# Placing turns and laid rows between the last modes' products, and sending the last rows of all batches but the first by DMA

## The chip, the cores and the metric

The kernel runs on one core of one Trainium2 chip. The metric is device time in microseconds (us), the median of several executions. Engines: PE multiplies matrices, DVE and ACT move and change data, POOL issues the loads of weights and the small copies, SP issues the output.

## The reference, cut to what matters

```python
# sliding-window attention, 8 batches x 8 heads x 576 rows x 64 -> x [8, 576, 512]
X = rfft(x, axis=1)                       # first 64 modes are kept
Yr = Xr[m] @ w_r[m] - Xi[m] @ w_i[m]      # per mode m: two 512 x 512 weights
Yi = Xr[m] @ w_i[m] + Xi[m] @ w_r[m]
y = irfft(Y, n=576, axis=1)
u = x + y
out = u + relu(u @ w_ch)                  # w_ch 512 x 512
```

The weights of the 64 modes are 134 MB in float32. They are read once, and the transfer casts them to bfloat16 (512 KB each in memory on the chip).

## The kernel before

Modes 0 to 59 go through `mode()`. The last four, 60 to 63, are treated apart so that little remains to be done after the last weight: their products go to `psl`, eight rows a batch. The spectrum of each batch is 128 rows: 96 early ones, 24 *middle rows* (modes 48 to 59) and 8 *last rows* (modes 60 to 63). A *turn* (`turned`) multiplies such rows by `w_ch` into `psw` and transposes them into `psa`. In the closing stage each of 36 output tiles gets a *laid row* (`lay`: an identity product that puts the channel product of x into PSUM), a product with `yw`, a relu on ACT, a product with `Yb`, and an addition on DVE. `idle` products compute nothing that is used; they keep PE streaming, for the sake of its clock.

```python
def turned(lhs, m, psa, psw):
    for e in range(NC):
        nc.tensor.matmul(out=psw[:m, :], lhsT=lhs(e), rhs=wch[:, e, :], start=(e == 0), stop=(e == NC - 1))
    for e in range(NC):
        nc.tensor.transpose(out=psa[:m, e, :], in_=lhs(e), identity=ident_r)
# ... cut ...
        for b0, nb in ((2, 4), (6, 2)):                     # middle rows, all before the last modes
            psa = ...; psw = ...                            # one buffer each
            turned(lambda e: view(YTl, (e * B + b0) * R, [[1, R * nb]]), R * nb, psa, psw)
            for i in range(nb):                             # DVE empties psa, ACT empties psw
                nc.vector.tensor_copy(out=pair_tile("Yb", b0 + i)[E0:], in_=...)
                nc.scalar.copy(out=pair_tile("yw", b0 + i)[E0:], in_=...)
        for n in range(EARLY_ROWS):                         # 5
            lay(n)
        for m in range(ME, NM):                             # modes 60 to 63
            last_mode(m, wr, 0, 0, NC)                      # 16 products
            idle(5 if m < NM - 1 else 3)
            last_mode(m, wi, 1, 0, NC)                      # 16 products
            if m < NM - 1:
                idle(5)
# ... cut: closing stage: YT2 <- psl, one turn of batches 0 and 1 and the last rows of 2 to 7 ...
        RELU = 3
        for n in range(RELU):
            rectify(n)                                      # product with yw, relu
        for n in range(NQ):
            finish(n)                                       # product with Yb, addition, output
            if n < 2:
                spread(n)                                   # ACT copies psw / psa to yl, DMA to batches 2 to 7
            if n + RELU < NQ:
                rectify(n + RELU)
            if EARLY_ROWS <= n + RELU + 1 < NQ:
                lay(n + RELU + 1)
```

The softmax here doesn't subtract the row's maximum and nothing guards it: scores larger than these inputs give would overflow.

## Time and profile before

| | before |
|---|---|
| time, median of 3 (later 4) runs | 432.32 (432.34) us |
| last piece of the last weight has landed | 392.76 us |
| its last 16 products end (`psl` done) | 394.90 us |
| first product of the turn of the last rows | 395.56 us |
| first product of the closing stage | 397.41 us |
| PE's last product | 425.29 us |
| end of the span | 431.94 us |

Times inside a kernel are counted from the start of the profiled span. Landing times are the semaphore records of the trace: a load is landed when the last of its 16 engines has reported.

From the page: the span; the clock that PE was granted, in tenths of full speed; the busy share of the DMA engines. Both rows have 40 slices of 10.8 us.

```profile
span 431.9 us, 11402 instructions
...
PEclk9999999999998755555588998996566655569998
DMA  7999999999999999999999999999999999991897
```

DMA is above 90% in every slice from the 2nd to the 36th: until about 389 us the kernel is a stream of weights. After that comes the closing stage, which writes 9.4 MB.

PE in order of time, around the end of the stream (start, length, line, operation, output <- inputs; in brackets the idle time before and what ended it):

```profile
374.75 2.08 PE L678 MATMUL psw<-wch,YTl 128*128 128x512 f32 x4 [0.68 <-ACT YTl L58]
...
379.25 1.97 PE L678 MATMUL psw<-wch,YTl 128*64 128x512 f32 x4 [1.96 <-ACT yw L748]
...
383.69 0.68 PE L720 MATMUL psl<-XQ,wt 128*128 128x16 bf16 x16
384.21 1.37 PE L693 MATMUL psd<-x_sb,ident_bf 128*128 128x512 bf16 x5
...
394.27 0.63 PE L720 MATMUL psl<-XQ,wt 128*128 128x16 bf16 x16
...
397.41 0.96 PE L793 MATMUL pso<-yw,trigI 128*128 128x512 f32 x3 [0.39 <-ACT yw L777]
```

All turns and laid rows stand before 383.69. Then halves of last modes (16 products, 0.48 us to the next instruction) alternate with idle products (five take 1.08 us). None of the lines from 383.69 to 394.27 has a bracket, so PE waits for no weight there. The weights landed at these times, us:

```
mode 60: 375.46, 377.92   mode 61: 380.38, 382.89   mode 62: 385.29, 387.75
mode 63: 390.20, then the last weight in three pieces: 391.49, 392.11, 392.76
```

The last half starts 1.5 us after its data was complete. The chain of waits (start, length, what) says the same: after the load that ends at 373.03 there is no DMA left in it, only PE and, after `psl`, two copies one after the other.

```profile
355.11 17.92 DMA wt<-in_moe_w_i_dram
...
393.78 0.65 PE psd L693 x3
394.43 0.48 PE psl L720 x16
394.94 0.24 DVE YT L767
395.19 0.33 ACT YT L769
395.56 1.20 PE psw L678 x4
```

Stretches of the trace, here three: length, then busy time and count of PE, PE's weight loads, DVE, ACT and POOL, then the granted clock, the DMA share and GB/s.

```profile
387.92:391.33 3.41, 3.41 (x45) 2.06 (x44) 0.00 (x0) 0.00 (x0) 0.00 (x0) 1.00 0.73 128
391.33:394.75 3.42, 3.42 (x59) 2.30 (x56) 0.00 (x0) 0.00 (x0) 0.00 (x0) 1.00 0.06 11
410.00:415.00 5.00, 5.00 (x23) 4.05 (x22) 4.50 (x7) 3.72 (x8) 0.00 (x0) 1.00 1.01 376
```

With five idle products between halves PE is busy all of the time and the clock stays at 1.00. The third line is the closing stage: PE is busy throughout, but the DMA share is 1.01 too.

### The profile page before, as it was taken

The numbers are of one execution on the slowest core, as the hardware profiler recorded it, in microseconds if no ns is written. First come the engines' busy times: TensorE is split into PE (matmuls) and PEld (weight loads), VectorE is DVE, ScalarE is ACT, GpSimd is POOL, SyncE is SP. The second block draws the span as 40 slices with busy tenths as digits, with TensorE's granted clock in tenths as the row PEclk, the third lists the DMA queues.
The fourth block names the chain that finished last, engine by engine and source line by source line (L and its number), as shares of the span: only waits on it lengthen the run. The fifth ranks groups of instructions, "written<-read, shape, count | busy, mean of one in ns | idle before, by whom it ended". The sixth has DMA issues, their size and how long they took to land.

```text
span 431.9 us, 11402 instructions
## 1 busy us (share of the span) xinstructions
PE 314.1 (73%) x5080; PEld 224.1 (52%) x5080; DVE 163.1 (38%) x316; ACT 152.3 (35%) x263; POOL 96.8 (22%) x184
## 2 busy tenths in 40 slices
PE   6989999999989756122777978785265662488993
PEld 2555765666655656122566756553254541355782
DVE  5466765766663200307122322221011110032894
ACT  4485866866764120101122321221011110122872
POOL 7131231331020404212121212122102131200500
PEclk9999999999998755555588998996566655569998
DMA  7999999999999999999999999999999999991897
GB/s 143 212 213 213 214 213 213 213 212 213 214 214 202 190 214 216 254 214 213 214 213 213 214 214 213 213 214 213 214 213 214 214 209 214 214 210 29 263 367 267
DMA packets 31314, 92.17 MB, mean 213 GB/s; under 512 B 3392, under 2 KB 3648, under 8 KB 31264
## 3 DMA queue, kind: packets, MB, share of 16 engines
q0 software_dynamic: 26016, 82.00, 95.6%
q1 hardware_dynamic: 5248, 9.44, 6.2%
q8 instruction: 40, 0.66, 0.5%
q14 instruction: 10, 0.08, 0.1%
HBM read 162.53 MB, written 9.44 MB: 398 GB/s over the span
## 4 chain that ended last, share of the span: by engine, by line
DMA 43%; PE 39%; DVE 6%; issue 4%; ACT 3%; POOL 2%; DVEq 0%; POOLq 0%; ACTq 0%
DMA wt<-in_moe_w_r_dram 27%; DMA wt<-in_moe_w_i_dram 17%; PE pso L317 6%; PE pst L219 6%; PE pso L793 4%; PE psv L236 3%; PE psx L339 3%; DVE x_sb L325 2%; PE pss L372 2%; PE pss L273 2%; PE pso L714 2%; PE pss L292 2%; PE psy L551 2%; PE psy L546 2%; DVE vT L59 2%
## 5 line engine op out<-in xcount | busy, mean ns | idle before, releaser
L551 PE MATMUL psy<-XQ,wt 128*128 128x16 bf16 x784 | 48.1, 191 | 48.0 <-DMA wt<-in_moe_w_i_dram 46.4
L546 PE MATMUL psy<-XQ,wt 128*128 128x16 bf16 x832 | 52.3, 191 | 31.9 <-DMA wt<-in_moe_w_r_dram 31.3
L551 PEld LDWEIGHTS <-wt 128*128 128x128 bf16 x784 | 37.2, 104 | 54.2 <-DMA wt<-in_moe_w_i_dram 51.5
L546 PEld LDWEIGHTS <-wt 128*128 128x128 bf16 x832 | 39.6, 104 | 37.2 <-DMA wt<-in_moe_w_r_dram 36.0
L116 POOL DMA_DIRECT2D wt<-in_moe_w_i_dram x53 | 28.7, 542 | 101.1 <-DMA wt<-in_moe_w_i_dram 40.1
L572 PE MATMUL psz<-wch,xT 128*128 128x512 f32 x144 | 47.7, 474 | 1.0 <-DVE xT L569 1.0
L116 POOL DMA_DIRECT2D wt<-in_moe_w_r_dram x55 | 29.7, 539 | 78.8 <-DMA wt<-in_moe_w_r_dram 43.9
L569 DVE CAST xT<-pxt 128x512 fp32r<-128x512 bf16 x36 | 23.5, 687 | 62.4 <-PE pxt L566 62.4
L574 ACT CAST Z<-psz 128x512 fp32r<-128x512 f32 x36 | 21.1, 587 | 70.9 <-PE psz L572 70.8
L298 ACT ACTIVATE et<-pss 128x512 bf16<-128x512 f32 x72 | 39.2, 599 | 12.7 <-PE pss L292 12.6
L317 PE MATMUL pso<-vt,et 128*64 128x65 bf16 (+1 forms) x576 | 33.1, 204 | 4.3 <-DVE x_sb L325 4.2
L572 PEld LDWEIGHTS psz<-wch,xT 128*128 128x128 f32 x144 | 30.4, 226 | 7.2 <-issue 1.3
L317 PEld LDWEIGHTS <-et 128*64 128x64 bf16 (+1 forms) x576 | 22.9, 109 | 15.8 <-issue 7.8
L325 DVE TENSOR_TENSOR x_sb<-pso,rcp 128x640 bf16<-128x640 f32 x32 | 26.3, 822 | 0.9
L804 DVE TENSOR_TENSOR ot<-pso,x_sb 128x512 f32<-128x512 f32 x36 | 24.5, 691 | 2.5 <-PE pso L793 2.0
L59 DVE CAST YT<-psy 128x256 fp32r<-128x256 f32 x6 | 2.5, 423 | 59.8 <-PE psy L551 59.8
L798 ACT ACTIVATE pso<-pso 128x512 f32<-128x512 f32 x36 | 20.5, 582 | 5.4 <-PE pso L793 2.9
L273 PE MATMUL pss<-band,ident_bf 64*64 64x512 bf16 x160 | 19.9, 391 | 1.6 <-ACT et L298 1.6
L58 ACT CAST YT<-psy 128x256 fp32r<-128x256 f32 x6 | 2.2, 374 | 51.5 <-DVE YT L59 51.5
L59 DVE COPY vT<-pst 128x768 bf16<-128x768 bf16 x16 | 15.3, 958 | 13.4 <-PE pst L219 13.4
L686 DVE CAST Yb<-psa 96x512 fp32r<-96x512 f32 x8 | 5.5, 687 | 32.5 <-PE psa L680 32.5
L678 PE MATMUL psw<-wch,YT 128*96 128x512 f32 (+1 forms) x36 | 16.4, 601 | 0.7 <-ACT YT L769 0.7
(167 smaller groups left out, 509.0 us busy)
## 6 DMA issues: line engine op xcount, KB each, us to landing
wt<-in_moe_w_r_dram POOLq DMA_DIRECT2D x55, 512.0 KB, 19.1
wt<-in_moe_w_i_dram POOLq DMA_DIRECT2D x50, 512.0 KB, 19.1
out_dram<-ot SPq DMA_DIRECT2D x32, 256.0 KB, 3.2
rk<-in_k_dram POOLq DMA_DIRECT2D x8, 576.0 KB, 9.2
rq<-in_q_dram POOLq DMA_DIRECT2D x8, 576.0 KB, 13.3
rv<-in_v_dram POOLq DMA_DIRECT2D x8, 576.0 KB, 11.8
wy<-in_moe_w_i_dram POOLq DMA_DIRECT2D x4, 512.0 KB, 16.3
kT<-in_moe_w_i_dram POOLq DMA_DIRECT2D x2, 512.0 KB, 7.0
```

Of the source, the lines that this page charges most:

```text
L59: return nc.vector.tensor_copy(out=o, in_=i)
L116: nc.gpsimd.dma_start(out=wt[:, c0:c1], in_=src[m].rearrange("(p c) e -> p c e", c=NC)[:, c0:c1])
L219: nc.tensor.transpose(out=ps[64 * hh:64 * hh + 64, c, :], in_=src[:, hh, (c0 + c) * D:(c0 + c + 1) * D], identity=ident_bf)
L273: nc.tensor.matmul(out=pss[(2 * w + hh) % 3][64 * half:64 * half + 64, :], lhsT=ident_bf[pp, pp], rhs=view(band[pp], 128 * half, [[0, WIN ...
L298: nc.scalar.activation(out=et[:, hh, :], in_=pss[(2 * w + hh) % 3], func=ACT_F.Exp, scale=EX_SCALE)
L317: nc.tensor.matmul(out=pso[po, hh, (i // 2) * VW:(i // 2) * VW + D + 1], lhsT=et[pk, hh, col:col + 64], rhs=vt[pk, 1 - f % 2, 2 * hh + g / ...
L325: nc.vector.tensor_tensor(out=view(x_sb, b * NT * DM + g * D, [[4 * D, 2], [DM, NT], [1, D]]), in0=view(pso, 0, [[512, 2], [VW, NT], [1, D]]),
L546: nc.tensor.matmul(out=psy[:, m % MG, e, :], lhsT=wr[:, c, ee], rhs=XQ[:, c, :, 1:3, m], start=(c == 0), stop=(m == 0 and c == NC - 1))
L551: nc.tensor.matmul(out=psy[:, m % MG, e, :], lhsT=wi[:, c, ee], rhs=XQ[:, c, :, 0:2, m], start=False, stop=(c == NC - 1))
L569: nc.vector.tensor_copy(out=xT, in_=pst)
L572: nc.tensor.matmul(out=psz, lhsT=xT[:, c, :], rhs=wch[:, c, :], start=(c == 0), stop=(c == NC - 1))
L804: nc.vector.tensor_tensor(out=ot, in0=tps.pop(n), in1=x_sb[:, b, t, :], op=ALU.add)
```

## The change

The intent: let PE do turns and laid rows while it waits for weights, so that it is on time for the last one; make the step after `psl` shorter (one copy in place of two on different engines); take copies off ACT in the closing stage by treating batch 1 as batches 2 to 7; and load the last weight at once, as PE no longer needs its pieces. The number of idle products falls from 33 to 11.

```diff
@@ -112,8 +112,7 @@
         if wt is None:
             wt = pool.tile([128, NC, DM], BF16, name="wt", tag=tag)
         src = moe_w_i if im else moe_w_r
-        for c0, c1 in ((0, NC),) if i < NLOAD - 1 else ((0, 2), (2, 3), (3, 4)):
-            nc.gpsimd.dma_start(out=wt[:, c0:c1], in_=src[m].rearrange("(p c) e -> p c e", c=NC)[:, c0:c1])
+        nc.gpsimd.dma_start(out=wt, in_=src[m].rearrange("(p c) e -> p c e", c=NC))
         wtiles[m, im] = wt
 
     trigF = acons.tile([128, NT, 2 * NM], BF16, name="trigF")
@@ -735,10 +734,10 @@
                 free.extend([(wy, j, NM) for j in range(3)])
                 refill_w(m)
 
-        YT2 = wlate.tile([128, NC, 128], FP32R, name="YT2", tag="wl")
-        nc.vector.tensor_copy(out=view(YT2, 0, [[128, NC], [R, 2], [1, R - RL]]),
-                              in_=view(YTl, 0, [[B * R, NC], [R, 2], [1, R - RL]]))
-        for b0, nb in ((2, 4), (6, 2)):
+        YT2 = wlate.tile([128, NC, 96], FP32R, name="YT2", tag="wl")
+        nc.vector.tensor_copy(out=YT2[:, :, 0:R - RL], in_=YTl[:, :, 0, 0:R - RL])
+
+        def middle_rows(b0, nb):
             psa = ps_a.tile([128, NC, 128], FP32R, name="psa", tag="psa")
             psw = ps_a.tile([128, DM], FP32, name="psw", tag="psw")
             turned(lambda e: view(YTl, (e * B + b0) * R, [[1, R * nb]]), R * nb, psa, psw)
@@ -746,16 +745,29 @@
                 nc.vector.tensor_copy(out=pair_tile("Yb", b0 + i)[E0:],
                                       in_=psa[R * i:R * i + R].rearrange("p c e -> p (c e)"))
                 nc.scalar.copy(out=pair_tile("yw", b0 + i)[E0:], in_=psw[R * i:R * i + R, :])
-        for n in range(EARLY_ROWS):
+
+        psl = ps_l.tile([128, NC, RL * B], FP32, name="psl", tag="psl")
+
+        def last(m, im):
+            last_mode(m, wtiles.pop((m, im)), im, 0, NC)
+
+        middle_rows(1, 4)
+        last(ME, 0)
+        lay(0)
+        lay(1)
+        last(ME, 1)
+        middle_rows(5, 3)
+        last(ME + 1, 0)
+        for n in range(2, EARLY_ROWS):
             lay(n)
-        psl = ps_l.tile([128, NC, RL * B], FP32, name="psl", tag="psl")
-        for m in range(ME, NM):
-            wr, wi = wtiles.pop((m, 0)), wtiles.pop((m, 1))
-            last_mode(m, wr, 0, 0, NC)
-            idle(5 if m < NM - 1 else 3)
-            last_mode(m, wi, 1, 0, NC)
-            if m < NM - 1:
-                idle(5)
+        last(ME + 1, 1)
+        last(ME + 2, 0)
+        idle(4)
+        last(ME + 2, 1)
+        idle(4)
+        last(ME + 3, 0)
+        idle(3)
+        last(ME + 3, 1)
 
     wl.close()
     p3 = p2.enter_context(ExitStack())
@@ -764,27 +776,27 @@
 
     with tc.manual_schedule(engines={mybir.EngineType.PE, mybir.EngineType.Activation, mybir.EngineType.DVE,
                                      mybir.EngineType.Pool, mybir.EngineType.SP}):
-        nc.vector.tensor_copy(out=view(YT2, R - RL, [[128, NC], [R, 2], [1, RL]]),
-                              in_=view(psl, 0, [[RL * B, NC], [RL, 2], [1, RL]]))
-        nc.scalar.copy(out=view(YT2, 2 * R, [[128, NC], [1, RL * (B - 2)]]),
-                       in_=view(psl, 2 * RL, [[RL * B, NC], [1, RL * (B - 2)]]))
+        nc.vector.tensor_copy(out=YT2[:, :, R - RL:R - RL + RL * B], in_=psl)
         psa = ps_a.tile([128, NC, 128], FP32R, name="psa", tag="psa")
         psw = ps_a.tile([128, DM], FP32, name="psw", tag="psw")
-        NR = 2 * R + RL * (B - 2)
+        NR = R + RL * (B - 1)
         turned(lambda e: YT2[:, e, 0:NR], NR, psa, psw)
         flat = psa.rearrange("p c e -> p (c e)")
         yl = yp.tile([128, 2, DM], FP32R, name="yl")
+
+        def send(i, b):
+            r0 = R + RL * (b - 1)
+            nc.gpsimd.dma_start(out=pair_tile(("yw", "Yb")[i], b)[128 - RL:], in_=yl[r0:r0 + RL, i])
+
         nc.scalar.copy(out=pair_tile("yw", 0)[E0:], in_=psw[0:R])
+        nc.vector.tensor_copy(out=yl[0:NR, 0], in_=psw[0:NR])
+        send(0, 1)
         nc.vector.tensor_copy(out=pair_tile("Yb", 0)[E0:], in_=flat[0:R])
-        nc.vector.tensor_copy(out=pair_tile("yw", 1)[E0:], in_=psw[R:2 * R])
-        nc.vector.tensor_copy(out=pair_tile("Yb", 1)[E0:], in_=flat[R:2 * R])
-
-        def spread(i):
-            src = flat if i else psw
-            nc.scalar.copy(out=yl[2 * R:NR, i], in_=src[2 * R:NR])
-            for b, j in ((2, 0), (3, 0)) if i == 0 else ((2, 1), (3, 1)) + tuple((b, j) for b in range(4, B) for j in range(2)):
-                r0 = 2 * R + RL * (b - 2)
-                nc.gpsimd.dma_start(out=pair_tile(("yw", "Yb")[j], b)[128 - RL:], in_=yl[r0:r0 + RL, j])
+        nc.vector.tensor_copy(out=yl[0:NR, 1], in_=flat[0:NR])
+        send(1, 1)
+        for b in range(2, B):
+            for i in range(2):
+                send(i, b)
 
         def add(n, what, stop):
             b, t = seq[n]
@@ -810,8 +822,6 @@
             rectify(n)
         for n in range(NQ):
             finish(n)
-            if n < 2:
-                spread(n)
             if n + RELU < NQ:
                 rectify(n + RELU)
             if EARLY_ROWS <= n + RELU + 1 < NQ:
```

## The prediction

> **What bounds it.** Until 392.8 us the kernel waits for weights. The chain of waits is DMA from 355.1 to 373.1 us; each mode's two 512 KB loads land 2.45 us apart (landing records: 375.46, 377.92, 380.38, 382.89, 385.29, 387.75, 390.20; the last weight in three pieces at 391.49, 392.11 and 392.76). From 374.75 us on, PE is the chain (timeline of PE): turns of the middle rows 374.75 to 377.3 and, after a 1.96 us wait for ACT to empty psw, 379.25 to 381.65; five laid rows to 383.7; then eight halves of last modes (0.48 us each) with 5 or 3 idle products between (1.08 to 1.21 us), ending at 394.90. The last half starts loading at 394.05, 1.3 us after its data landed: in this stretch PE is late, not DMA. The closing stage (397.4 to 425.3) is PE-bound, three or four products of 0.23 us a tile.
>
> **What the change does.**
> 1. Turns and laid rows go between the last modes' products, so PE does this work while weights arrive. My sum: first turn to 377.3, modes 60 to 61 with rows and second turn to about 384, then each half waits for its weight. The last half follows DMA: one load should land at 390.20 + 2.45 = 392.65, its 16 products end about 0.85 us later (as 394.05 to 394.90 now), near 393.5. Gain 1.35 us. One load saves 0.1 us of transfer but loses the start on early pieces; about zero.
> 2. After psl, DVE then ACT copied in turn (394.94 to 395.52). One DVE copy of 256 columns should take 0.42 us (the 128x256 YT cast). Gain 0.15 us.
> 3. Closing stage: ACT loses two 0.58 us copies, which held PE up at 400.8, 401.4 and 402.0 (0.2 to 0.3 us each on PE, 1 us with what follows). DVE's three evacuations stay three (0.69 us), in another order. Against that, batch 1's last rows now come by DMA: yl copy 0.7 us after psw, then 2.6 us from issue to landing (first such DMA now, 400.40 to 403.03). PE's fifth rectify product waits until 3.4 us after psw instead of 2.64; by its eighth the two kernels are level. Net zero.
>
> So 1.5 us off if the clock holds.
>
> **The clock.** The trace's clock records change only in steps of 3.41 us, between 0.5 and 1.0; the Trainium skill, "TensorE: Matmul & The Clock Gate", Part 1, tells of a free-running window of that length, and the trace agrees. Working out streamed columns per window, the clock fell in windows below about 0.37 and rose above 0.65 to 0.8. Before, five idle products kept 0.78 to 0.81. After, four idle products and one half stream 0.96 us of each 2.45 us: 0.39, right at the edge, with gaps of about 1 us. In many window phases the clock will fall near 385 us, and the closing stage may begin at half clock for 2 to 4 us, costing 1 to 2.5 us. That varies from run to run. Estimated mean cost: 0.6 to 1 us.
>
> **Predicted:** 431.4 us, 80% range 429.9 to 432.9. Faster by over 2%: 1%; within 2%: 98%; slower by over 2%: 1%.
>
> **What would show it.** Step 1: PE idle just before the last three halves, waiting on DMA, and psl complete near 393.5 us. Step 2: psl to first psw product 0.5 us instead of 0.66. Step 3: PE waiting for a yw DMA once, about 0.8 us; no later wait. Clock: dips to 0.5 between 384 and 398 us, and wider spread of times.
>
> **What would make it wrong.** A clock low through the start of the closing stage (slower, up to 433.5); batch 1's DMA landing later than 4 us under output traffic; the YT2 buffer or psa coming free late, so the second turn passes 386 us.

## The result, and the profile after

After: 431.23 us median (430.95 to 432.28, 4 runs); before: 432.34 us (432.08 to 432.92, 4 runs). The ratio is 0.9977, 95% interval 0.9957 to 0.9997: some 1 us faster, which counts as the same at 2%. A ratio is the mean time of one kernel's fast runs over that of the other's of the same rounds, so it is not quite the ratio of the medians.

Between the two profiled executions the span shrank by 2.68 us, from 431.94 to 429.26. This is where it went:

| stretch | before | after | difference |
|---|---|---|---|
| start to end of mode 59 | 374.07 | 373.31 | -0.76 |
| end of mode 59 to last landing | 18.69 | 18.67 | -0.02 |
| last landing to `psl` done | 2.14 | 0.69 | -1.45 |
| `psl` done to first product of the turn | 0.66 | 0.52 | -0.14 |
| turn to first product of the closing stage | 1.85 | 2.04 | +0.19 |
| first to last product of the closing stage | 27.88 | 27.99 | +0.11 |
| PE's last product to the end | 6.65 | 6.05 | -0.60 |

The first line is not the change's doing. The instruction order of the two programs was compared engine by engine, and it differs nowhere before mode 59's end. Later executions put that moment anywhere between 372.67 and 374.98 us. The last line, -0.60, stays unexplained; the experiments come back to it. So the unit of comparison below is the time from the last landing on.

The page after:

```profile
span 429.3 us, 11354 instructions
...
PEclk9999999999998555555588988959556665586997
DMA  7999999999999999999999999999999999993798
```

The clock row has changed near its end, 6 6 5 5 8 6 9 9 7 in place of 6 5 5 5 6 9 9 9 8: it now dips again where the closing stage begins.

PE after, in order of time:

```profile
376.33 0.68 PE L719 MATMUL psl<-XQ,wt 128*128 128x16 bf16 x16
...
378.51 1.18 PE L677 MATMUL psw<-wch,YTl 128*96 128x512 f32 x4 [0.45 <-ACT yw L747]
...
382.20 0.65 PE L719 MATMUL psl<-XQ,wy 128*128 128x16 bf16 x16 [0.98 <-DMA wy<-in_moe_w_i_dram]
384.62 0.65 PE L719 MATMUL psl<-XQ,wy 128*128 128x16 bf16 x16 [1.77 <-DMA wy<-in_moe_w_r_dram]
385.11 1.87 PE L692 MATMUL psd<-x_sb,ident_bf 128*128 128x512 bf16 x4
...
392.02 0.64 PE L719 MATMUL psl<-XQ,wt 128*128 128x16 bf16 x16 [0.95 <-DMA wt<-in_moe_w_i_dram]
...
396.75 0.77 PE L805 MATMUL pso<-Yb,trigI 128*128 128x512 f32 x1
...
398.01 0.50 PE L805 MATMUL pso<-yw,trigI 128*128 128x512 f32 x1
```

The first half (376.33) comes straight after the first turn; the second turn (378.51) waited 0.45 us for ACT to empty `psw`, in place of 1.96. From 382.20 on each half starts 0.04 to 0.05 us after its weight has landed (382.15, 384.57, 387.04, 389.48, 391.97): DMA sets the pace, also where no bracket shows a wait because idle products filled it. For the last half that delay was 1.51 us before.

The chain of waits after:

```profile
374.02 17.95 DMA wt<-in_moe_w_i_dram
...
392.02 0.66 PE psl L719 x16
...
392.70 0.44 DVE YT L779
...
393.18 1.40 PE psw L677 x4
```

DMA is in the chain up to 391.97, as it should be. The one copy from `psl` takes 0.44 us, where two took 0.24 and 0.33 with a gap between.

Stretches after, cut at the moments when the clock could change:

```profile
380.31:383.73 3.42, 1.56 (x24) 0.96 (x20) 1.96 (x4) 1.15 (x2) 0.00 (x0) 1.00 1.07 216
383.73:387.14 3.41, 2.41 (x22) 0.95 (x23) 0.00 (x0) 0.00 (x0) 0.00 (x0) 0.50 1.06 213
387.14:390.55 3.41, 3.33 (x38) 1.58 (x39) 0.00 (x0) 0.00 (x0) 0.00 (x0) 0.50 0.79 159
390.55:393.97 3.42, 1.95 (x23) 1.08 (x21) 0.43 (x1) 0.00 (x0) 0.00 (x0) 1.00 0.09 18
393.97:397.38 3.41, 3.17 (x11) 1.96 (x10) 2.06 (x3) 1.90 (x4) 0.52 (x1) 0.50 0.03 4
```

The clock falls at 383.73, comes back at 390.55, falls at 393.97 (the closing turn is then 1.4 us long in place of 1.2) and is at 1.00 from 397.38. The prediction had such dips. The next three lines show what it did not have. DVE and POOL after, in order of time:

```profile
395.20 0.69 DVE L792 CAST yl<-psw 88x512 fp32r<-88x512 f32 x1 [2.08 <-ACT yw L791]
395.92 0.68 DVE L794 CAST Yb<-psa 32x512 fp32r<-32x512 f32 x1
```

```profile
396.18 0.52 POOL L789 DMA_DIRECT2D yw<-yl  x1 [21.62 <-DVE yl L792]
```

DVE's first `yl` copy did not start when `psw` was ready (394.56). It waited for ACT's copy of the same bank, and ran from 395.20 to 395.89. The DMA of batch 1's last rows was issued at 396.18 and landed at 397.97; PE's fifth `yw` product started at 398.01.

### The profile page after: what moved, and what is told of

Same layout as the page of the kernel before. It is cut to its first block, busy times and chain, and to the rows that moved or that the text cites. A ratio compares the mean times of both kernels' runs of the same rounds, so it can differ in the third digit from the quotient of the medians.

```text
span 429.3 us, 11354 instructions
## 1 busy us (share of the span) xinstructions
PE 312.6 (73%) x5058; PEld 223.1 (52%) x5058; DVE 164.0 (38%) x317; ACT 151.6 (35%) x261; POOL 96.6 (23%) x184
## 4 chain that ended last, share of the span: by engine, by line
DMA 46%; PE 36%; DVE 7%; issue 5%; ACT 2%; POOL 2%; DVEq 0%; POOLq 0%; SPq 0%; ACTq 0%
DMA wt<-in_moe_w_r_dram 30%; DMA wt<-in_moe_w_i_dram 16%; PE pso L316 6%; PE pst L218 6%; PE pso L805 4%; PE psv L235 3%; PE psx L338 3%; DVE x_sb L324 2%; PE pss L272 2%; PE pss L371 2%; PE pss L291 2%; PE psy L545 2%; PE psy L550 2%; DVE vT L59 2%; PE pso L713 1%
## 5 line engine op out<-in xcount | busy, mean ns | idle before, releaser
L115 POOL DMA_DIRECT2D wt<-in_moe_w_i_dram x51 | 27.8, 544 | 99.8 <-DMA wt<-in_moe_w_i_dram 43.2
L115 POOL DMA_DIRECT2D wt<-in_moe_w_r_dram x55 | 29.6, 539 | 78.6 <-DMA wt<-in_moe_w_r_dram 44.2
```

The lines of the kernel that those rows point to most:

```text
L115: nc.gpsimd.dma_start(out=wt, in_=src[m].rearrange("(p c) e -> p c e", c=NC))
```

## The experiments

Theory A, at the outset: the gain is PE being on time for the last weight, about 1.5 us, and a closing stage that begins at half clock gives some of it back. Rivals: the interleaving is needed in itself (B); the half clock costs nothing, as something else sets the closing stage (C); the new closing stage brings the gain by freeing ACT (D).

These runs (e1 to e4 on one chip, e5 to e12 on another) were noisier than the first result: the kernel before took 431.58 to 437.6 us in its fast runs there, and the intervals of the ratios are 0.25 to 0.5% wide on each side. Differences of 0.2% can't be settled by those times. All outputs were correct.

All stretches in us; "clock" is the granted clock when the closing stage's first product starts. `land` is the last landing, `psl` its products' end, `turn` the first product of the last turn, `first` and `last` PE's first and last product of the closing stage, `end` the end of the span. In e12 the clock fell 0.04 us after that first product; it is listed with the half clock that the stage then had.

| run | land to psl | psl to turn | turn to first | first to last | land to last | last to end | land to end | clock |
|---|---|---|---|---|---|---|---|---|
| before | 2.14 | 0.66 | 1.85 | 27.88 | 32.54 | 6.65 | 39.18 | 1.0 |
| after | 0.69 | 0.52 | 2.04 | 27.99 | 31.24 | 6.05 | 37.29 | 0.5 |
| e1 before, 3 idle | 0.33 | 0.67 | 1.84 | 27.90 | 30.74 | 6.54 | 37.28 | 1.0 |
| e2 after, more idle | 0.68 | 0.52 | 1.81 | 28.00 | 31.02 | 6.78 | 37.79 | 1.0 |
| e3 after, no idle | 0.67 | 0.61 | 2.64 | 28.00 | 31.92 | 6.24 | 38.16 | 0.5 |
| e4 after, old closing | 0.69 | 0.67 | 2.56 | 28.21 | 32.13 | 5.73 | 37.86 | 0.5 |
| e5 before, new closing | 2.00 | 0.52 | 1.82 | 27.99 | 32.33 | 6.37 | 38.71 | 1.0 |
| e6 after, pieces | 0.33 | 0.52 | 2.67 | 28.31 | 31.83 | 6.28 | 38.11 | 0.5 |
| e7 after, mended closing | 0.69 | 0.52 | 1.82 | 27.24 | 30.27 | 6.41 | 36.68 | 1.0 |
| e8 all three | 0.34 | 0.52 | 1.82 | 27.23 | 29.91 | 6.92 | 36.84 | 1.0 |
| e9 after, copy on ACT | 0.69 | 0.52 | 2.03 | 27.89 | 31.13 | 6.03 | 37.16 | 0.5 |
| e10 e1 + mended closing | 0.33 | 0.52 | 2.37 | 27.30 | 30.51 | 6.66 | 37.17 | 0.5 |
| e11 after again | 0.69 | 0.52 | 1.82 | 28.00 | 31.03 | 6.19 | 37.22 | 1.0 |
| e12 all three again | 0.34 | 0.51 | 1.83 | 28.21 | 30.89 | 6.83 | 37.72 | 0.5 |

### Fewer idle products, nothing moved (e1)

```diff
 # kernel before
-            idle(5 if m < NM - 1 else 3)
+            idle(3)
-                idle(5)
+                idle(3)
```

> Kernel before with 3 idle products wherever it has 5; nothing moved. Theory A (the gain comes from PE no longer being late when the last weight lands, however that is brought about): PE's sum is 383.7 + 8 x 0.48 + 21 x 0.216 = 392.0 us less the last half, so the last half waits for its weight (392.8 us), psl is done near 393.5 and the time falls by about 1.0 to 1.4 us to 431.0 (ratio 0.997), as much as the whole change. Rival B (the interleaving itself is needed): no gain, ratio 1.000 +- 0.001.

Measured: 432.92 us median, before 434.09 in the same rounds, ratio 0.9984 (0.9944 to 1.0025), which decides nothing by itself. The profile decides. PE around the last weight:

```profile
390.53 0.39 PE L720 MATMUL psl<-XQ,wt 128*128 128x16 bf16 x8
391.11 0.29 PE L720 MATMUL psl<-XQ,wt 128*128 128x16 bf16 x4 [0.19 <-DMA wt<-in_moe_w_i_dram]
391.75 0.29 PE L720 MATMUL psl<-XQ,wt 128*128 128x16 bf16 x4 [0.35 <-DMA wt<-in_moe_w_i_dram]
```

PE is early: the last half begins at 390.53 and waits for each of the last two pieces. Landing to the end is 37.28 us, against 37.29 after the whole change and 39.18 before. Up to PE's last product e1 is even 0.5 us better than after (30.74 against 31.24 us). Rival B falls: 33 idle products of 0.216 us (7.1 us, worked out from the five in 1.08 us) stood between the halves, and taking 12 of them away (2.6 us) makes PE as punctual as moving the turns did. PE's 1.96 us wait for ACT before the second turn is longer than the lateness too; no run removes that wait alone.

### More idle products (e2), none (e3)

```diff
 # kernel after, before each of the last four halves:   e2          e3
-        (none), idle(4), idle(4), idle(3)
+        idle(5), idle(6), idle(6), idle(5)           # e2
+        (none)                                       # e3
```

> Kernel after with 5, 6, 6, 5 idle products before the last four halves in place of 0, 4, 4, 3. Theory A (the closing stage starts at half clock and gives back about 1 us): 6 products and a half stream 0.57 of each 2.45 us, the clock stays at 1.0 up to the closing stage, from the last weight's landing to PE's last product takes 30.3 us in place of 31.2, time 430.3 us (ratio to before 0.9955). Rival C (the closing stage is set by batch 1's DMA, the half clock there is hidden behind it): within 0.3 us of after (431.2).

> Kernel after without idle products. Theory A: a half streams only 0.04 of each 2.45 us, so the clock is at 0.5 from about 385 us until 397 to 401 us; the closing stage loses 1 to 2 us more than in after, time 432 to 433.5 us. Rival C (half clock hidden): within 0.3 us of after (431.2).

Measured: e2 431.35 us median, ratio 0.9954 (0.9929 to 0.9979); e3 431.86 us, ratio 0.9980 (0.9942 to 1.0019). In e2 the clock stayed at 1.0 from 377.0 us to the end of the closing stage, in e3 it was 0.5 from 388.4 to 398.6 us. The turn shows it: 1.81 us to the first closing product in e2, 2.64 in e3. But the closing stage itself takes 28.00 us in both (e3 has half clock for its first 1.1 us), and 27.99 in after with half clock for its first 2.2 us. Theory A expected 30.3 us from landing to the last product in e2; it is 31.0. So rival C is right for these closing stages, and theory A for the turn before them. The ratio of e2 fits theory A's 0.9955 all the same, but its profile does not bear that reason out: landing to end is 37.79 us, 0.5 longer than in after. What hides the half clock there is in e2's timeline of PE:

```profile
394.36 0.96 PE L806 MATMUL pso<-yw,trigI 128*128 128x512 f32 x3 [0.41 <-ACT yw L792]
395.89 0.47 PE L806 MATMUL pso<-Yb,trigI 128*128 128x512 f32 x1 [0.57 <-DVE Yb L795]
...
397.17 0.50 PE L806 MATMUL pso<-yw,trigI 128*128 128x512 f32 x1 [0.35 <-DMA yw<-yl]
```

At full clock PE is done sooner and then stands still: the first `Yb` product waits for DVE's `Yb` copy (which comes after the late `yl` copy), and the fifth `yw` product waits for the DMA of batch 1's last rows.

### The closing stage of before in the new kernel (e4), and the new one in the old kernel (e5)

```diff
 # e4: kernel after with
-        middle_rows(1, 4) ... middle_rows(5, 3)
+        middle_rows(2, 4) ... middle_rows(6, 2)
+        # YT2 of 128 columns, filled by DVE and then ACT; batches 0 and 1 evacuated directly; spread(n) for n < 2
 # e5: kernel before with the closing stage of after, and
-        for b0, nb in ((2, 4), (6, 2)):
+        for b0, nb in ((1, 4), (5, 3)):
```

> Kernel after with the closing stage of before: batches 0 and 1 evacuated directly, YT2 filled by DVE and then ACT, two spread copies on ACT; interleaving, idle products and single load as in after. Theory A: the new closing stage is worth 0.15 us for the one copy and about zero for the rest, so 431.2 to 431.5 us. Rival D (the new closing stage brought the gain by freeing ACT): 432.2 us or more, as before.

> Kernel before (turns and laid rows ahead of the last modes, 5 idle products, last weight in pieces) with only the closing stage of after. Theory A (only PE's lateness was worth anything; the two closing stages are level at full clock): PE still late, its last half about 1.3 us after the landing, clock 1.0, first closing product to PE's last product 28.0 us as in after and in the run with more idle products (27.9 before), landing to PE's last product 32.4 us (32.5 before), time within 0.3 us of before. Rival D (new closing stage brought the gain): 31.5 us or less.

Measured: e4 431.45 us median, ratio 0.9972 (0.9938 to 1.0006); e5 434.31 us, ratio 1.0015 (0.9966 to 1.0064). In e5 the last half started 1.37 us after the landing, and landing to PE's last product is 32.33 us, 0.2 under before and 1.1 over after. So the new closing stage brings next to nothing of itself, and rival D falls. In e4 `psl` to turn is back at 0.67 us, which confirms the one copy's 0.15 us. The old closing stage takes 27.88 us at full clock (before), 27.90 (e1), and 28.21 where it began at half clock (e4): there 1.1 us of half clock cost about 0.3 us. In the new one up to 2.2 us cost nothing; e6 below, whose clock was 0.5 until 400.68 us, 3.6 us into its closing stage, takes 28.31 us, 0.3 more than e2, e5 and e11 at full clock.

### The last weight in pieces again (e6)

```diff
 # kernel after
-        nc.gpsimd.dma_start(out=wt, in_=src[m].rearrange("(p c) e -> p c e", c=NC))
+        for c0, c1 in ((0, NC),) if i < NLOAD - 1 else ((0, 2), (2, 3), (3, 4)):
+            nc.gpsimd.dma_start(out=wt[:, c0:c1], in_=src[m].rearrange("(p c) e -> p c e", c=NC)[:, c0:c1])
```

> Kernel after with the last weight in three pieces again. The prediction's 'about zero' for the single load: landing to the end of psl stays 0.69 us. The run of before with 3 idle products shows another value, 0.33 us, as 12 of the 16 products were done before the last piece landed; if that is the pieces' doing, landing to the end of psl is 0.33 us here, and landing of mode 59 to the last landing stays within 0.1 us of 18.67 us. Time 0.3 us under after.

Measured: 433.16 us median, ratio 0.9978 (0.9931 to 1.0024). Landing to `psl` is 0.33 us, as expected, because 12 of 16 products are done before the last piece lands. The pieces take 2.55 to 2.56 us from the landing of the weight before them (all seven runs that have them), the single load 2.45 to 2.51 (the other seven). So the single load gives up 0.36 us to save about 0.07. One expectation was missed: mode 59 to last landing was 19.84 us in place of 18.67. The delay is not in the pieces; the weight of mode 62 landed 3.5 us after its predecessor in this execution, where 2.45 us is usual. A smaller one, 2.9 to 3.1 us, was seen between 382 and 387 us in e2, e4, e5, e8, e11 and e12 too, single load or not; its cause is open.

### The closing stage mended (e7), the copy alone (e9)

```diff
 # e9: kernel after with
-        nc.vector.tensor_copy(out=yl[0:NR, 0], in_=psw[0:NR])
+        nc.scalar.copy(out=yl[0:NR, 0], in_=psw[0:NR])
 # e7: the same, and rows 6 to 8 laid in PE's early waits
         for n in range(RELU):
             rectify(n)
+        lay(5)
         for n in range(NQ):
             finish(n)
+            if n == 1:
+                lay(7)
             if n + RELU < NQ:
                 rectify(n + RELU)
+            if n == 0:
+                lay(6)
-            if EARLY_ROWS <= n + RELU + 1 < NQ:
+            if EARLY_ROWS + 3 <= n + RELU + 1 < NQ:
                 lay(n + RELU + 1)
```

> Kernel after with the closing stage mended: the copy of psw to yl goes from DVE to ACT right after ACT's yw copy (DVE had to wait for ACT's copy of the same bank), DVE starts with Yb at once; rows 6 to 8 are laid in PE's three early waits. Theory E (the closing stage's 28.0 us is set by DVE's late yl copy and the DMA behind it, not by the clock): waits of PE in the closing stage fall from 2.0 to about 1.0 us, first product to last 26.9 to 27.2 us, time 0.8 to 1.1 us under after: 430.3 us. Rival: DMA under output traffic or the ACT engine's extra copy gives the time back, 27.8 us or more.

> Kernel after with only the copy of psw to yl moved from DVE to ACT (rows laid as in after). Theory E in two parts: at full clock the wait before the first finish falls from 0.72 to 0.38 us and that for batch 1's DMA from 0.51 to about 0.4 us, so PE's waits are 1.6 us in place of 2.0 and first to last product 27.5 to 27.6 us; laying rows 6 to 8 early is worth the other 0.35 us (27.24 in the mended closing stage). If the copy's place brought all of it: 27.2; if none: 28.0.

Measured: e7 431.43 us median, ratio 0.9961 (0.9919 to 1.0003); e9 431.0 us, ratio 0.9992 (0.9947 to 1.0036). PE's early closing stage in e7:

```profile
396.67 0.40 PE L713 MATMUL pso<-Z,ident_r 128*128 128x512 f32 x1
397.03 0.50 PE L805 MATMUL pso<-Yb,trigI 128*128 128x512 f32 x1
...
398.55 0.50 PE L805 MATMUL pso<-yw,trigI 128*128 128x512 f32 x1
```

The laid row at 396.67 stands where PE waited for the first relu, the first `Yb` product follows 1.17 us after the first `yw` product (1.53 in e2), and first to last product is 27.24 us. The expected 430.3 us was missed, and the times do not separate e7 from after. In the profile, 0.76 us of the closing stage are gone at the same clock as in e2 and e11: PE's early waits had a part in its 28.0 us. But e7 does two things at once, an earlier copy and rows laid in the waits, and no run lays the rows alone. How much of it is the copy's place alone e9 can't tell: its clock was 0.5 until 397.1 us, and at half clock the two early waits are, as far as can be argued, covered by PE's own slowness (27.89 us against 27.99 in after in the same clock state). Its expectation of 27.5 us was for full clock and stays untested.

### All three together (e8, again in e12), and without the interleaving (e10); after again (e11)

```diff
 # e8, e12: e7 + last weight in pieces (as e6) + 5, 6, 6, 5 idle products (as e2)
 # e10: e5 + 3 idle products everywhere (as e1) + closing stage of e7
 # e11: kernel after, unchanged
```

> The mended closing stage, the last weight in three pieces, and 5, 6, 6, 5 idle products (clock held). If the three add: landing to first closing product 2.7 us (3.25 in after), first to last product 26.9 us (28.0 in after), landing to PE's last product 29.6 us against 31.2 in after and 32.5 before; time 429.6 us or a ratio of 0.9935 to before.

> No interleaving: turns, then all laid rows, then last modes with 3 idle products, weight in pieces, and the mended closing stage. Rival B' (once PE is no longer late, interleaving is worth nothing): clock 1.0 into the closing stage, landing to psl 0.34, landing to first closing product 2.7 us, first to last product 27.2 us, landing to PE's last product 29.9 us as in the run with all three (interleaved). If interleaving is worth something of itself, 30.5 us or more.

> Kernel after itself, for comparison on the same chip, and for what the clock does in another phase of its windows: first to last product within 0.4 us of 28.0 us whatever the clock; landing to first product 3.0 us if the clock is 1.0 when psl is done, up to 3.9 us if it is 0.5. Ratio to before 0.9965 to 0.998.

> The run with all three (mended closing stage, pieces, more idle products) once more, beside after on the same chip: landing to PE's last product 29.9 us +- 0.2; 1.0 to 1.8 us under after in the fast runs' mean, ratio to before 0.994 to 0.9965, if the chip is quiet enough to tell.

Measured: e8 432.4 us median, ratio 0.9968 (0.9923 to 1.0012); e10 430.62 us, ratio 0.9962 (0.9930 to 0.9994); e11 432.01 us, ratio 1.0010 (0.9965 to 1.0055); e12 430.77 us, ratio 0.9965 (0.9934 to 0.9996). The last three and e9 ran in the same rounds, where before had a median of 433.09 us. By their times none of e7, e8, e10 and e12 can be told from after.

e11 is the same kernel as after, with the clock at 1.0 when `psl` was done: landing to PE's last product 31.03 us against 31.24. So the half clock cost after 0.2 us in the profiled execution, all of it in the turn. Its ratio of 1.0010 missed the expectation of 0.9965 to 0.998. Two of its six fast runs took over 436 us, and the interval holds both answers.

e8 reaches 29.91 us from landing to PE's last product, 2.6 less than before and 1.33 less than after. That is the sum of the three parts as measured one by one (0.36 pieces, 0.76 closing stage, 0.21 clock), if not the expected 29.6. e12 is the same kernel and reaches only 30.89. Its clock fell at 394.2 us, just as the closing stage began:

```profile
390.82:394.20 3.38, 2.08 (x21) 1.28 (x17) 0.83 (x2) 0.62 (x2) 0.00 (x0) 1.00 0.02 3
394.20:397.60 3.40, 3.40 (x8) 2.73 (x9) 1.66 (x3) 2.49 (x5) 2.58 (x6) 0.50 0.10 15
```

PE was busy for 2.08 of 3.38 us in that stretch, and the stage after it ran at half clock: 28.21 us in place of 27.23. Once PE's early waits are mostly gone, 3.4 us of half clock cost 1.0 us; product by product, all of it is lost in the first 5 us. In e10 the clock fell at 393.0 us, earlier: the turn took 0.5 us longer, the closing stage, with 1.4 us of half clock, only 27.30 us. Those 0.5 us of the turn make up most of what e10's 30.51 us lie above its expected 29.9. That e10 would equal e8 at the same clock, without any interleaving, is argued from this and not shown.

Not all that PE gains reaches the end. From landing to the end of the span e8 gains 0.45 us on after, where PE gains 1.33: the time after PE's last product is 6.92 us in place of 6.05. It was 6.83 in e12 and 6.19 in e11, so it goes with the kernel. In these profiles SP issues its last output 1.8 (e8), 1.7 (e12), 1.5 (after) and 1.3 us (e11) after DVE's last addition. The outputs queue, with the DMA share near 1.0 from 405 us on. Which part is the queue and which the chance of an execution stays open.

## Why the prediction was right or wrong

The time was right: 431.4 us predicted, 431.23 measured, within the range and within 2%. Point by point:

1. *PE late, not DMA.* Right. "Gain 1.35 us": landing to `psl` fell from 2.14 to 0.69 us, 1.45 us. What the prediction did not say is that the interleaving is one of two ways to get there; e1 gets it by deleting idle products. Of the waits that it named before the last three halves the trace shows one (0.95 us, before the last); at half clock the idle products filled the other two.
2. *The single load: "about zero".* Wrong in size. It saved about 0.07 us of transfer, as said (0.1), but the lost early start is worth 0.36 us (0.69 against 0.33 us from landing to `psl` in e6). The term is a loss of about 0.3 us.
3. *One copy, "gain 0.15 us".* Right: 0.66 to 0.52 us, the copy 0.43 us long against 0.42 predicted.
4. *Closing stage, "net zero".* Right in sum (27.99 against 27.88 us), and the wait came at the named product and time: 3.4 us after `psw` both predicted and measured. About 0.8 us of waiting was named: the weight load of that product waited 0.47 us for the DMA in after and 0.77 us at full clock in e2. But two terms were off and cancelled. The `yl` copy was to end 0.7 us after `psw` and ended 1.33 us after it, since DVE waited for ACT's copy of the same bank. The DMA was to take 2.6 us and took 1.79. It was the first of its kind with little other traffic; the 2.6 us had been read from one among output. The Trainium skill, "DMA: Bandwidth & Descriptors", section "Anatomy of one DMA — SWDGE (gpsimd) path", fits one DMA on this path as 2.0 us and the bytes over 436 GB/s, which makes an estimate of 2.04 us for these 16 KB; the 1.79 us here are near it, and 4.4 us, the longest of after, are not. The late `Yb` copy, which makes PE wait 0.7 us at full clock (e2: the third `yw` product starts 0.57 us after the first and takes 0.2 us, the `Yb` product starts at 1.53), was not foreseen at all.
5. *The clock.* The mechanism was right: it fell at 383.7 and at 394.0 us, and the closing stage began at half clock. It did not fall after the windows with four idle products (0.39 by the prediction), though, but after 380.31 to 383.73, where PE had no idle products and waited for weights, and after 390.55 to 393.97, which holds the wait for the last weight and the gap before the turn; by the estimate of the last section, matmuls streamed for 0.21 and 0.30 of these windows. (The same estimate gives 0.77 and 0.78, not 0.78 to 0.81, for the five idle products of before.) The size, "costing 1 to 2.5 us" and 0.6 to 1 us in the mean, was too high: 0.2 us in the profiled execution (31.24 against 31.03 us in e11). One execution is no mean. Six traces have after's idle products; against the same stages at full clock, turn and closing stage lost 0.2 us in after, 1.0 in e4, 1.2 in e6, at least 0.2 in e9, and nothing in e7 and e11, an estimated 0.4 us in the mean. The step that failed is the assumption that PE's products are what the first 3 us of the closing stage wait for. They wait for DVE and DMA there: up to 2.2 us of half clock cost the closing stage nothing (e3, after), 3.6 us cost 0.3 (e6), and 3.4 us cost 1.0 once the waits are mended (e12 against e8). Most of the rest is lost in the turn, up to 0.85 us (e6).
6. *Wider spread of times.* 1.3 us from lowest to highest after, 0.8 before, in four runs each: too few to say.

That the total still fitted is partly luck. The predicted 0.9 us is 1.5 less a clock cost that was too high. From landing to PE's last product after gained 1.30 us in its profile, and 1.51 in e11.

## What to carry to other kernels

When an engine is late at the end of a stream, first add up what stands in its queue by choice: here 7.1 us of clock-keeping products stood before a half that was 1.5 us late, and removing a third of them was worth as much as a rearrangement. Where a stage begins with evacuations that others wait for, check which engine reads which PSUM bank in what order, since one engine's copy can hold back the other's and the DMA behind it. And a slow clock costs little where the engine is not what the stage waits for: mend the other waits and it costs more.

## What the Trainium skill lacked or had wrong

- "TensorE: Matmul & The Clock Gate", Part 1, names the 3.41 us window, and the trace agrees: each of its clock records, but those cut by the ends of the trace, lasts a multiple of 3.41 us. But the page has the clock fall after an idle window ("Why this matters for your kernels" asks for no idle gap over about 3 us); its section "A second HAM failure mode: psum-queue depth-cycling" has frequent short idle times do it too, and gives no share. Here it fell with PE busy for 2.08 of 3.38 us and no gap over 0.6 us (e12). The share of a window that matmuls stream was estimated for all 14 traces, in all windows between 215 and 396 us: the columns of the moving operands over the page's 2.4 GHz times the granted clock, with the idle products whose own record is missing put in where their weight load stands. That window of e12 has 0.34. At full clock it fell after 112 of 114 windows with a share of 0.33 or less, after 24 of 44 from 0.34 to 0.38, and after none of 188 from 0.39 on.
- The same page has sustained matmuls raise the clock. In the kernel before, products of 16 columns kept PE busy for nearly all of 147 to 154 us, and the clock stayed at 0.5; by the same estimate they stream 0.46 of a window. In the same count it rose after none of 226 windows up to 0.65, after 15 of 42 from 0.66 to 0.78, and after 114 of 115 from 0.79 on.
- "DMA: Bandwidth & Descriptors" says that engines 7 and 15 are usually slower than the others. Here the 16 engines of one 512 KB load reported over 3.1 us (after) and 3.9 us (before), longer than the 2.45 us from one load to the next, so the last engines to report set when a weight is usable; the records do not say which these are. The page gives no size for this.
